# Another order for the end of the kernel stage: the last direct term on GpSimd, weight columns split ahead of the norm and behind it

## The chip, the cores and the metric

One Trainium2 chip, one of its cores. The metric is the device time of one run in microseconds (us); lower is better. The kernel before takes 1165.28 us, the median of three runs (1164.83 to 1167.33).

Engines go by the names of the profile: PE is TensorE (matmul), PEld its weight loads, DVE is VectorE, ACT is ScalarE, POOL is GpSimd, SP is SyncE, which here issues nearly all transfers (DMAs). Each engine works through a queue of its own in order: an instruction that waits holds up all that stand behind it on its engine.

## The reference

Two layers, each of a state-space convolution and a gated feed-forward part, over 2048 positions of 512 channels, with a residual around each part:

```python
def _A_ref(u, A_re, A_im, B_re, B_im, C_re, C_im, log_dt, Dskip):
    dt = jnp.exp(log_dt)[:, None]
    A = A_re + 1j * A_im
    ...
    P = jnp.exp(logdA[:, :, None] * l[None, None, :])
    K = jnp.einsum("dn,dnl,dn->dl", Cc, P, dB).real
    ...
    Yf = Uf * Kf[None, :, :, :]
    ...
    y = (lambda x, *d: x.transpose(*d))(y, 0, 2, 1) + u * Dskip[None, None, :]
    return y
def _B_ref(x, w_gate, w_up, w_down):
    g = _silu(x @ w_gate)
    u = x @ w_up
    return (g * u) @ w_down
x = A_u
x = x + _A_ref(_layernorm(x, axis=-1), ...)
x = x + _B_ref(_layernorm(x, axis=-1), ...)
```

The last two lines stand there twice, for the two layers, with the same parameters. `K` is the convolution's kernel over the 2048 positions, the same for both layers; `u * Dskip` is its direct term.

## The kernel before, in words

The positions are cut into four blocks of 512. The convolution of a block is a product of spectra: a Fourier transform of each block in four groups of frequencies `q` (taken in the order 0, 3, 1, 2) and two halves `h` of the channels, so eight pieces (h, q) per block; block `b` sums the products of its blocks 0 to `b` with the spectra of `K`. The feed-forward part (`ffn`) takes 256 positions at a time, in f16 pairs: every weight is split into a high half and a low half, and each product is three matmuls (lines 909, 910, 912 for gate and up, 924 to 926 for down).

**The kernel stage** comes first (about 0 to 319 us). It makes `K` in eight chunks of 64 channels, and beside it the spectra, the largest column sums of the weights and the first blocks' transforms. Its end, behind the last chunk's matmuls, is written out by hand: inside a `manual_schedule` block the program order is the queue order on ACT, DVE, PE and POOL. The change is in this part. What it consists of:

- `lags` (L491 to L498): the last chunk's matmuls into `pk`. ACT copies them out as `ks` (`spread_in`, L507), PE spreads them into `kp` (`spread_pe`, L523), ACT copies that to the table `kt` (L525), and `skip` (L503) adds the direct term, 64 numbers on one partition, to `kt`. `first_parts` (L580) and `later_parts` (L531, ACT L598/L599, DVE L600, store L538) turn `kt` into spectra.
- `conv[0]`, `conv[1]`: the first block's convolution, one generator per half, five steps and a sixth. Each of the first four steps is one piece q: DVE multiplies (`yk`, L776) and combines (`yf`, L781, L782), PE transforms back (`pi`, L796, eight records of matmuls), and ACT (L748) or DVE (L756, L757) adds pieces up in `bb`. The fifth step makes rows 0 and 1 of the block (L811 to L816), the sixth rows 2 and 3 (L820 to L827). The spectra of half 1 are loaded into `u4` piece by piece (L713), each as soon as `yk` has read the piece of half 0 that lay there.
- `scales()` (L344 to L356, eleven small DVE instructions): from the weights' column sums the powers of two, `sc6`, by which they are split.
- `split(hi, lo, load)`: the split of the weights. `load` issues the next load (L660 for a quarter of the columns of gate or up, 688 KB; L683 and L685 for rows of down), `hi` makes the next high half on ACT (L664; L689 for down), `lo` the next low half on DVE (L669; L692 for down). The quarters come as gate 0, up 0, gate 1, up 1, and so on. A loaded quarter lies in a borrowed buffer until both halves are made; the list `tags` in `split_weights` says in which: `"bt"`, `"n"` or `"xf"`, or a slot 0 to 2 in `wsl[3]`, whose memory the last chunk's matmuls read until they end.
- `norm`: the first feed-forward norm (`first_norm`): statistics on DVE (L203 to L205), a power on POOL (L206), the scaling (L841) on ACT, eight transposes on PE (L843), and the copies L846 (ACT) and L848 (DVE).
- `second(...)`, `direct`: the transform of one piece of the second block for later (16 matmul records at L296, ACT L299, store L300).

Behind the block the order of every engine is set by a scheduler that works from priorities. There the rest of the split stands (`while los`), then for each of the eight (layer, block) pairs the next block's convolution and this one's `ffn`. The first `ffn` multiplies with columns 0 to 255 (f0=0), 256 to 511 (f0=2), and so on; each group's result `pgu` lies in one of two banks of accumulators until ACT (L915, `silu`) and DVE (L916) have read it.

## Time and profile before

| | us |
|---|---|
| median of three runs | 1165.28 |
| the profiled execution | 1163.68 |
| its span in the trace | 1161.5 |
| PE busy in the span | 1099.4 |
| DVE busy | 1000.5 |
| ACT busy | 594.4 |
| POOL busy | 109.1 |
| first matmul of the feed-forward part (L909) | at 318.98 |

A line of the trace's timeline reads: start in us, length in us, engine, line, operation, output and inputs by the program's names, the shapes, the count; in brackets the idle time of the engine just before and what ended it. Instructions of one engine overlap a little, so a line's length is somewhat more than the distance to the next. An f32 matmul stands in the records twice. In a table by stretches each engine's busy time is given with the number of its records, then the granted TensorE clock (1.00 is full), the share of the transfer engines and their GB/s.

### The profile page before, as it was taken

To read this page: it belongs to the slowest core of one execution; us is meant where nothing else is said; L and a number is where in the kernel's file an instruction comes from. 1 tells how busy PE (TensorE), PEld (TensorE's weight loads), DVE (VectorE), ACT (ScalarE), POOL (GpSimd) and SP (SyncE) were. 2 spreads that over 40 slices of the span, in tenths; PEclk is the share of its full clock that TensorE was granted. 3 is DMA by queue.
4 is the path that set the end of the run, shared out by engine and by line. 5 is a ranking of instruction groups with operands and counts; after the bars stand their busy time and mean duration, and the time that the engine had idled before them with its cause. 6 is when DMAs were issued, how large, how long until landed. Compare 5 with 4: busy or idle time off the path is not lost.

```text
span 1161.5 us, 24413 instructions
## 1 busy us (share of the span) xinstructions
PE 1099.4 (95%) x9948; PEld 875.2 (75%) x9948; DVE 1000.5 (86%) x1593; ACT 594.4 (51%) x1194; POOL 109.1 (9%) x162
## 2 busy tenths in 40 slices
PE   1979999998889999999999999999999999999998
PEld 1868888886777868687868687868777686876875
DVE  7999999978889999999899999989994999983212
ACT  6689888833553463557453533655433452334211
POOL 0112222210000010010010000210000010000000
PEclk9989999999989999999999999999999999999999
DMA  5356777766493437332254454342534145312000
GB/s 208 118 148 171 171 176 163 187 184 221 124 290 120 144 119 223 104 111 74 79 154 135 126 162 143 103 131 89 164 110 150 49 121 153 107 42 46 15 24 19
DMA packets 127314, 150.38 MB, mean 129 GB/s; under 512 B 50897, under 2 KB 75985, under 8 KB 127202
## 3 DMA queue, kind: packets, MB, share of 16 engines
q1 hardware_dynamic: 115298, 123.32, 35.0%
q0 software_dynamic: 11904, 25.50, 9.5%
q8 instruction: 78, 1.28, 0.5%
q14 instruction: 34, 0.28, 0.1%
HBM read 98.70 MB, written 33.82 MB: 114 GB/s over the span
## 4 chain that ended last, share of the span: by engine, by line
PE 33%; DVE 26%; issue 8%; DMA 4%; ACT 3%; SPq 1%; POOL 1%; DVEq 0%; ACTq 0%; POOLq 0%
PE pgu L909 6%; PE pgu L910 5%; PE pgu L912 5%; DVE t L776 4%; DVE yk L779 4%; PE py L924 3%; PE py L925 3%; PE py L926 3%; DVE yk L776 3%; DVE z L228 2%; PE pi L796 2%; PE pf L280 2%; DVE sg L916 2%; DVE hl L918 1%; DMA mix<-nn 1%
## 5 line engine op out<-in xcount | busy, mean ns | idle before, releaser
L909 PE MATMUL pgu<-mix,wsl 128*128 128x256 f16 x1280 | 300.1, 274 | 5.5 <-DVE sg L916 4.6
L910 PE MATMUL pgu<-mix,wsl 128*128 128x256 f16 x1280 | 299.7, 274 | 0.0
L912 PE MATMUL pgu<-mix,wsl 128*128 128x256 f16 x1280 | 195.6, 274 | 0.0
L910 PEld LDWEIGHTS <-wsl 128*128 128x128 f16 x1280 | 125.7, 98 | 22.7 <-issue 6.3
L924 PE MATMUL py<-wsl,hh 128*128 128x512 f16 (+1 forms) x352 | 133.4, 379 | 4.7 <-DVE xg L929 3.0
L909 PEld LDWEIGHTS <-wsl 128*128 128x128 f16 x1280 | 125.7, 98 | 16.2
L912 PEld LDWEIGHTS <-wsl 128*128 128x128 f16 x1280 | 125.7, 98 | 15.3
L926 PE MATMUL py<-wsl,hl 128*128 128x512 f16 (+1 forms) x352 | 133.4, 379 | 0.5 <-DVE hl L918 0.5
L925 PE MATMUL py<-wsl,hh 128*128 128x512 f16 x320 | 121.3, 379 | 0.0
L776 DVE TENSOR_TENSOR t<-uu,w 128x1024 f32<-128x1024 f32 x96 | 116.9, 1217 | 3.5 <-DMA w<-wdr 3.3
L915 ACT ACTIVATE sg<-pgu,sc 128x512 f32<-128x512 f32 x80 | 54.6, 683 | 126.5 <-PE pgu L912 123.3
L779 DVE TENSOR_TENSOR yk<-yk,t 128x1024 f32<-128x1024 f32 x96 | 116.8, 1217 | 0.2
L916 DVE SCALAR_TENSOR_TENSOR sg<-pgu,sc,sg 128x512 f32<-128x512 f32 x80 | 59.7, 746 | 52.2 <-ACT sg L915 52.0
L531 PE MATMUL pw<-kt,ek 128*128 128x256 f32 (+1 forms) x384 | 91.0, 374 | 0.0
L917 ACT ACTIVATE hh<-sg 128x512 f16<-128x512 f32 x80 | 50.1, 627 | 77.8 <-DVE sg L916 77.8
L796 PE MATMUL pi<-yl,mix 128*128 128x256 f16 x576 | 78.9, 272 | 0.6 <-DVE yl L228 0.3
L531 PEld LDWEIGHTS pw<-kt,ek 128*128 128x128 f32 x384 | 72.5, 193 | 8.6
L280 PE MATMUL pf<-z,eh 128*128 128x256 f16 x576 | 74.9, 273 | 0.6 <-DVE z L228 0.6
L776 DVE TENSOR_TENSOR yk<-u,w0r 128x1024 f32<-128x1024 f32 x56 | 68.2, 1217 | 0.8 <-ACT u L282 0.8
L918 DVE TENSOR_TENSOR hl<-sg,hh 128x512 f16<-128x512 f32 x80 | 54.9, 686 | 15.5 <-ACT hh L917 15.4
L496 PE MATMUL pk<-re,g 128*32 128x64 f32 x1024 | 61.4, 300 | 6.7 <-DMA g<-g 3.3
L925 PEld LDWEIGHTS <-hh 128*128 128x128 f16 (+1 forms) x352 | 34.4, 98 | 41.5 <-issue 6.0
(237 smaller groups left out, 2162.3 us busy)
## 6 DMA issues: line engine op xcount, KB each, us to landing
w<-wdr SPq DMA_DIRECT2D x96, 256.0 KB, 2.8
uu<-udr SPq DMA_DIRECT2D x96, 256.0 KB, 3.0
udr<-u POOLq DMA_DIRECT2D x32, 256.0 KB, 2.6
g<-g POOLq DMA_DIRECT2D x6, 1024.0 KB, 9.1
udr<-u SPq DMA_DIRECT2D x16, 256.0 KB, 2.9
n<-xdr SPq DMA_DIRECT2D x4, 1024.0 KB, 5.7
kdr<-ks SPq DMA_DIRECT2D x6, 512.0 KB, 2.6
kt<-kdr SPq DMA_DIRECT2D x24, 128.0 KB, 2.9
```

Of the source, the lines that this page charges most:

```text
L280: PE.matmul(pf[:, o], lhsT=e, rhs=m, start=k == 0, stop=k == len(terms) - 1)
L531: PE.matmul(pw[:, i], lhsT=e, rhs=kt[:, :, c + 4 * k0:4 * k1:4, :].rearrange("p g k d -> p k g d"), start=c == 0, stop=c == 3)
L776: V.tensor_tensor(t, uu.unsqueeze(2).to_broadcast([P, NQ, 2, 2, DC]), w.unsqueeze(3).to_broadcast([P, NQ, 2, 2, DC]), OP.mult)
L779: V.tensor_tensor(yk, yk, t, OP.add)
L796: PE.matmul(pi[:, o], lhsT=e, rhs=m, start=k == 0, stop=k == len(terms) - 1)
L909: PE.matmul(o, lhsT=wgu(wi, k, 0)[:, fs], rhs=nh[:, k], start=k == 0, stop=False)
L910: PE.matmul(o, lhsT=wgu(wi, k, 1)[:, fs], rhs=nh[:, k], start=False, stop=False)
L912: PE.matmul(o, lhsT=wgu(wi, k, 0)[:, fs], rhs=nlo[:, k], start=False, stop=k == 3)
L916: V.scalar_tensor_tensor(sg, pgu[:, 1], sc6[:, 4:5], sg, OP.mult, OP.mult)
L924: PE.matmul(py[:, r], lhsT=hh[:n, f, rc], rhs=wd(f, 0)[:n], start=f == 0, stop=False)
L925: PE.matmul(py[:, r], lhsT=hh[:n, f, rc], rhs=wd(f, 1)[:n], start=False, stop=False)
L926: PE.matmul(py[:, r], lhsT=hl[:n, f, rc], rhs=wd(f, 0)[:n], start=False, stop=f == FT - 1)
```

## The change

The calls inside the hand-written part stand in another order. The additions are the same, apart from three things: `skip` of the last chunk goes to POOL (`G`) where it was on DVE (`V`); the second load (up 0) goes to the buffer `"n"`, so that only two loads need the memory of the last chunk's matmuls at first, and `bb1`, which takes the same buffer, is made later; and the eighth piece of `second` is taken inside `conv[1]` where it stood at the end. `scales()` and the first `hi` stand ahead of everything, gate 0 and up 0 are finished before the third step of `conv[0]`, and the low halves of gate 1 to up 3 stand behind the norm's statistics.

```diff
-        tags = iter(("bt", 0, 1, 2, "bt", 0, 1, 2, "n", "xf", "bt"))
+        tags = iter(("bt", "n", 0, 1, "bt", 2, 0, 1, "n", "xf", "bt"))
...
+        split(0, 0, 1)
         load_x(xs[0], 0, 0)
-        split(0, 0, 3)
+        split(0, 0, 2)
...
+        scales()
+        split(1, 0)
         ks = spread_in(pk)
...
-        bb1 = tl([P, 2, 2, 2, HD], "bb1", "n")
         norm = first_norm(tl([P, 2, D], "nn1", "hf"))
-        take(conv[0], 1)
-        spread_pe(ks, kts[1])
-        skip(c, kts[1], V)
-        take(conv[0], 1)
-        scales()
-        split(1, 0)
-        first_parts(c, 0)
-        take(conv[0], 1)
-        split(1, 1)
-        split(0, 0, 1)
-        first_parts(c - 1, 3)
+        last = second(*sec[-1])
         split(1, 0)
         take(conv[0], 1)
-        first_parts(c - 1, 1)
-        split(1, 0)
-        take(conv[1], 1)
-        first_parts(c, 2)
-        take(conv[1], 1)
+        split(0, 1)
+        split(0, 0, 1)
+        spread_pe(ks, kts[1])
+        skip(c, kts[1], G)
+        take(conv[0], 1)
         split(0, 1)
         split(0, 0, 1)
         take(conv[0], 1)
+        first_parts(c, 0)
+        split(1, 0)
+        bb1 = tl([P, 2, 2, 2, HD], "bb1", "n")
+        first_parts(c - 1, 3)
+        take(conv[0], 1)
+        first_parts(c - 1, 1)
         take(conv[1], 1)
-        split(1, 1)
-        split(0, 0, 1)
+        first_parts(c, 2)
+        split(1, 0)
         take(conv[1], 1)
-        split(0, 1)
-        split(0, 0, 1)
+        take(conv[0], 1)
+        take(conv[1], 1)
+        split(1, 0)
+        take(last, 2)
+        take(conv[1], 1)
         take(odd, 2)
         take(conv[1], 1)
         take(norm, 1)
+        split(0, 0, 1)
+        split(0, 1)
+        split(0, 0, 1)
         take(rest, 2)
...
         take(rest, 4)
+        split(0, 1)
         split(0, 0, 3)
         sizes(c, kts[1], ks)
         direct_size()
         nn2 = tl([P, 2, D], "nn2", "nn")
-        take(second(*sec[-1]), 2)
```

How this moves instructions is seen at three places. The first is DVE's queue from the last store of spectra (`wo`, L563) on, before:

```order
L563 TENSOR_TENSOR wo<-pw,wo 128x2x6x64
L776 TENSOR_TENSOR yk<-mix,w0r 128x1024
L781 TENSOR_TENSOR yf<-yk 128x256
L782 TENSOR_TENSOR yf<-yk 128x256
L503 TENSOR_TENSOR kt_438<-kt_438,tdk 1x4x16
L776 TENSOR_TENSOR yk<-mix,w0r 128x1024
L781 TENSOR_TENSOR yf<-yk 128x256
L782 TENSOR_TENSOR yf<-yk 128x256
L344 TENSOR_REDUCE c_2727<-cmx 128x3
```

and in the change, from the last instruction of `scales()` on, which now follow L563 at once:

```order
L356 TENSOR_SCALAR sc_92<-bits 128x6
L776 TENSOR_TENSOR yk<-mix,w0r 128x1024
L781 TENSOR_TENSOR yf<-yk 128x256
L782 TENSOR_TENSOR yf<-yk 128x256
L669 SCALAR_TENSOR_TENSOR wsl_2674<-st_2542,sc_92,wsl_2674 128x2x344
L669 SCALAR_TENSOR_TENSOR wsl_2675<-st_2542,sc_92,wsl_2674 128x2x344
L776 TENSOR_TENSOR yk<-mix,w0r 128x1024
L781 TENSOR_TENSOR yf<-yk 128x256
L782 TENSOR_TENSOR yf<-yk 128x256
L669 SCALAR_TENSOR_TENSOR wsl_2676<-st_2678,sc_92,wsl_2675 128x4x344
L776 TENSOR_TENSOR yk<-mix,w0r 128x1024
```

L503 is gone from DVE, and between the first, second and third piece of the convolution the low halves of gate 0 and up 0 are made.

The second place is PE's queue at the end of `conv[1]`; `pi` are its transforms, `pf` the sixteen matmuls of the eighth piece of `second`. The difference (a count of 4 is one piece):

```order
 L580 MATMUL pw<-kt_438,ef 128x64 x2
 L580 MATMUL pw<-kt_438,ek_84 128x64 x6
-L796 MATMUL pi<-yf,mix 128x256 x12
+L796 MATMUL pi<-yf,mix 128x256 x8
+L296 MATMUL pf<-n_1635,ef 128x256
+L296 MATMUL pf<-n_1635,ek_84 128x256
+L296 MATMUL pf<-n_1637,ek_84 128x256 x2
+L296 MATMUL pf<-n_1635,ef 128x256
+L296 MATMUL pf<-n_1635,ek_84 128x256
+L296 MATMUL pf<-n_1637,ek_84 128x256 x2
+L796 MATMUL pi<-yf,mix 128x256 x4
```

The `pf` matmuls now stand ahead of the convolution's last `pi`; before, they stood just ahead of the first matmul of the feed-forward part.

The third place is ACT's queue where the split of down (L689) meets the first `silu` (L915), set by the scheduler. Before:

```order
L222 ACTIVATE mv<-mv,epst 128x2
L689 ACTIVATE wsl_2677<-st_3036,sc_92 128x512 x4
L689 ACTIVATE wsl_2677<-st_3038,sc_92 128x512 x2
L689 ACTIVATE wsl_2677<-st_3038,sc_92 96x512
L860 ACTIVATE nn_3045<-xg,rs 128x512
L689 ACTIVATE wsl_2676<-st_3034,sc_92 128x512 x3
L689 ACTIVATE wsl_2677<-st_3034,sc_92 128x512
L915 ACT_TABLE_LOAD
L915 ACTIVATE sg_3081<-pgu,sc_92 128x512
```

and in the change:

```order
L689 ACTIVATE wsl_2677<-st_3051,sc_92 128x512 x2
L689 ACTIVATE wsl_2677<-st_3051,sc_92 96x512
L222 ACTIVATE mv<-mv,epst 128x2
L915 ACT_TABLE_LOAD
L915 ACTIVATE sg_3082<-pgu,sc_92 128x512
L689 ACTIVATE wsl_2677<-st_3049,sc_92 128x512 x4
L689 ACTIVATE wsl_2676<-st_3047,sc_92 128x512 x3
L689 ACTIVATE wsl_2677<-st_3047,sc_92 128x512
L915 ACTIVATE sg_3082<-pgu,sc_92 128x512
```

The first `silu` stood behind eleven high halves of down and now stands behind three. DVE's queue follows: ahead of its first L916 stood eleven low halves L692 and both L776 and L779 of the next block's first `k=1` term, and now three L692 and the L776. Further back the scheduler's order of the five engines differs in places up to matmuls that lie at about 598 us in the trace of before; from there to the end the rows of both programs are the same.

## The prediction

> **What bounds the kernel now.** I read the windows first: who is busy where.
>
> ```profile
> 260.00:280.00 20.00, 17.01 (x144) 14.25 (x137) 13.48 (x30) 7.89 (x9) 0.00 (x0) 0.91 0.82 287
> 280.00:300.00 20.00, 16.92 (x80) 14.40 (x79) 19.52 (x32) 5.25 (x10) 0.00 (x0) 0.83 0.45 132
> ...
> 340.00:440.00 100.00, 98.93 (x795) 74.69 (x794) 96.24 (x166) 44.89 (x89) 8.74 (x11) 1.00 0.45 134
> 440.00:545.00 105.00, 103.98 (x897) 83.64 (x895) 102.77 (x188) 55.91 (x109) 10.15 (x16) 1.00 0.40 126
> ```
>
> From 340 to 545 us PE idles 2.1 us (1.07 + 1.02) and DVE 6.0 us (3.76 + 2.23): both are full, and time won ahead of 340 stays won only if both win it. The end of the kernel stage, 260 to 334, is another matter. Next, therefore, PE's rows there; the bracket is its idle time and who ended it.
>
> ```profile
> 262.78 1.93 PE L523 MATMUL kp<-ks,ident 128*32 128x256 f32 x32
> 267.70 3.45 PE L796 MATMUL pi<-yf,mix 128*128 128x256 f32 x8 [2.99 <-DVE yf L781]
> ...
> 272.94 1.95 PE L796 MATMUL pi<-yf,mix 128*128 128x256 f32 x8
> ...
> 283.48 1.95 PE L796 MATMUL pi<-yf,mix 128*128 128x256 f32 x8
> 287.74 3.02 PE L796 MATMUL pi<-yf,mix 128*128 128x256 f32 x8 [2.31 <-DVE yf L781]
> 291.52 3.75 PE L796 MATMUL pi<-yf,mix 128*128 128x256 f32 x8 [0.77 <-ACT bb L748]
> ...
> 303.93 1.36 PE L843 MATMUL pt<-ident,nn 128*128 128x128 f32 x8 [3.33 <-ACT nn L841]
> 305.12 0.49 PE L531 MATMUL pw<-kt,ef 128*128 128x192 f32 x2
> ...
> 315.53 0.59 PE L296 MATMUL pf<-n,ef 128*128 128x256 f32 x2
> ...
> 318.98 0.27 PE L909 MATMUL pgu<-mix,wsl 128*128 128x256 f16 x1
> ...
> 333.97 0.37 PE L909 MATMUL pgu<-mix,wsl 128*128 128x256 f16 x1 [4.34 <-DVE sg L916]
> ```
>
> Five gaps, 13.7 us. Behind some of them matmuls take 1.6 to 1.9 times as long (`pi` 3.45, 3.02, 3.75 against 1.95). DVE's rows say why PE waits.
>
> ```profile
> 255.32 1.22 DVE L776 TENSOR_TENSOR yk<-mix,w0r 128x1024 f32<-128x1024 f32 x1
> ...
> 256.92 0.42 DVE L782 TENSOR_TENSOR yf<-yk 128x256 f32<-128x256 f32 x1
> 265.84 0.21 DVE L503 TENSOR_TENSOR kt<-kt,tdk 1x64 f32<-1x64 f32 x1 [8.51 <-ACT kt L525]
> ...
> 267.90 0.15 DVE L344 TENSOR_REDUCE c<-cmx 128x3 f32<-128x6 f32 x1
> ...
> 269.56 1.22 DVE L776 TENSOR_TENSOR yk<-mix,w0r 128x1024 f32<-128x1024 f32 x1
> ...
> 280.62 1.65 DVE L669 SCALAR_TENSOR_TENSOR wsl<-wsl,sc,wsl 128x1376 f16<-128x1376 f32 x1
> ...
> 301.08 0.17 DVE L205 TENSOR_SCALAR rs<-mv 128x2 f32<-128x2 f32 x1
> 301.17 1.78 DVE L669 SCALAR_TENSOR_TENSOR wsl<-st,sc,wsl 128x688 f16<-128x688 f32 x2
> ...
> 307.00 0.56 DVE L600 TENSOR_TENSOR wos<-pw,wos 128x384 f32<-128x384 f32 x1 [3.51 <-ACT wos L599]
> 308.96 0.56 DVE L600 TENSOR_TENSOR mix<-pw,mix 128x384 f32<-128x384 f32 x1 [1.40 <-ACT mix L599]
> ...
> 312.59 0.41 DVE L820 TENSOR_TENSOR bb<-bb 128x256 f32<-128x256 f32 x1
> ...
> 325.37 2.06 DVE L692 SCALAR_TENSOR_TENSOR wsl<-st,sc,wsl 128x512 f16<-128x512 f32 x3
> ...
> 333.17 0.75 DVE L916 SCALAR_TENSOR_TENSOR sg<-pgu,sc,sg 128x512 f32<-128x512 f32 x1
> ...
> 340.73 1.23 DVE L776 TENSOR_TENSOR t<-uu,w 128x1024 f32<-128x1024 f32 x1 [2.55 <-DMA w<-wdr]
> ```
>
> L503, 0.21 us of work, waits for ACT's `kt` and shuts DVE for 8.51 us while work that needs no `kt` stands behind it. From 312.59 DVE is full to its L916 at 333.17, for which PE waits 4.34 us.
>
> **The change part by part**, against the profiled execution (1163.68 us; the median of the runs shown is 1.6 us above it). ACT's rows:
>
> ```profile
> 261.02 1.02 ACT L507 ACTIVATE ks<-pk 128x1024 f32<-128x1024 f32 x1 [6.61 <-PE pk L497]
> ...
> 264.78 1.02 ACT L525 ACTIVATE kt<-kp 128x1024 f32<-128x1024 f32 x1 [1.30 <-PE kp L523]
> ...
> 269.73 1.44 ACT L664 ACTIVATE wsl<-st,sc 128x1376 f16<-128x1376 f32 x1 [3.93 <-DVE sc L356]
> ```
>
> *DVE's 8.51 us are filled.* From 255.4 on: `scales` 1.7 us (267.90 to 269.56), first piece 2.0 (255.32 to 257.34), gate 0's low half 1.7, second piece 2.0: `yf` at 262.8. PE then goes from `kp`, which ends at 264.71, straight into `pi` two. DVE waits 0.7 us for up 0's high half (ACT: L507 ends 262.04, plus 1.44), makes its low half (1.6), and the third piece is there at 267.1. On PE seven pieces, `pi` and L580 in turn, take 272.94 to 285.43, 1.78 us each. So: `pi` two to 266.5, nine pieces from 267.1 to 283.1, the moved `pf` 3.45 us (315.53 to 318.98), the last `pi` 1.95: end at 288.5, where it was 295.27. **The shift is 6.8 us**, with the 3.45 us of `pf` already done. DVE has 27.5 us of work to do meanwhile, is done at 285, and waits 3.5 us for that `pi`.
>
> *POOL's skip and the loads* hide behind this. No trace shows such an addition on POOL; the nearest rows:
>
> ```profile
> L223 POOL TENSOR_TENSOR rs<-mv,mhalf 128x2 f32<-128x2 f32 x15 | 24.6, 1637 | 176.1 <-ACT mv L222 176.1
> ...
> L206 POOL TENSOR_TENSOR rs<-rs,mhalf 128x4 f32<-128x4 f32 x2 | 2.0, 1020 | 33.0 <-DVE rs L205 33.0
> ```
>
> Bounds 0.2 us (DVE's price) and 1.64; I take 1.02, since it is as small an operation. `kt` is then there at 266.0 to 267.5; L580 wants it at 268.9, after `pi` three. Either end costs nothing; above 3 us PE waits. Behind it in POOL's queue stands only the norm's L206, wanted some 27 us later. The Trainium skill speaks against the move: "SBUF — State Buffer", Terms, says that VectorE and GpSimd share a port pair which one holds for its full instruction while the other is blocked. By that rule the addition could start up to one L776 (1.22 us) late, at worst to 268.7, still in time.
>
> Loads: four quarters and two blocks of x are now asked for within about 3 us of 261.
>
> ```profile
> L660 SPq DMA_DIRECT2D wsl<-in_B_w_up_dram x4: 383/460/1420, 261.4 to 295.7; - x4
> ...
> DMA to landing us min/median/max: 4.1/7.2/9.9
> ```
>
> At the longest, 9.9, gate 1 lands at 271.3; ACT takes it about 271.4. Up 0, asked for at 251.5, must be there at 262.0: 10.5 us. The same 9.9 for `u4`'s second piece, asked for at 263.1, gives 273.0, when DVE wants it at 272.7: I count 0.3. Later the loads of gate 3 and up 3 wait in SP's queue for the low halves of gate 1 and up 1 (about 296 and 298); behind them stand the stores of the L600, none of which is ready before 298, so nobody loses by it.
>
> *The norm.* L205, L669, L841 and L843 follow each other as before, so the transposes move by 6.9 us to 297.0 (L843 was 303.93), the eight L531 groups behind them still take 10.4 (305.12 to 315.53), and with `pf` gone the first L909 starts at **308.6 instead of 318.98**.
>
> *The first silu.* DVE reaches L600 at 302.0 (308.96 less 6.9) and, past L848, gate 2's low half and one L600, the block's second rows at 305.7 (as long as before, 3.6, since gate 2 replaces up 2). From there to L916 it took 20.6 (312.59 to 333.17); now up 2 is added (1.6), and eight L692 (0.67 each, 5.4), L779 (1.1) and 0.7 of small rows and waits fall away: 15.0. L916 runs at 320.7 to 321.4. PE, with two groups of 5.24 us done by 319.1, waits 2.3 us and starts f0=4 at **321.4 instead of 333.97, 12.5 us earlier**. ACT is in time: its three L689 and the table load fit ahead of 320.
>
> What such a gap does to the clock differs from case to case; the figure behind the counts of records is the granted clock:
>
> ```profile
> 304.00:306.00 2.00, 1.95 (x14) 1.72 (x15) 0.00 (x0) 1.25 (x2) 0.00 (x0) 1.00 0.82 199
> ...
> 334.00:336.00 2.00, 2.00 (x10) 1.44 (x10) 2.00 (x5) 1.88 (x3) 0.00 (x0) 0.50 1.64 170
> ```
>
> After the 4.34 us it was 0.50, after the 3.33 us ahead of the transposes 1.00. A cold start of f0=4 would cost up to about 2.6 us (half of 5.24). The Trainium skill's "TensorE: Matmul & The Clock Gate", Part 1, says that the clock halves after an idle window of about 3.4 us, so that by it a gap of 2.3 us stays warm; the trace doesn't bear it out, since 2.31 us of idle were followed by a `pi` of 3.02. The sum below holds with either, since PE isn't what sets it.
>
> *DVE sets it.* DVE idled 8.51 + 3.51 + 1.40 + 0.30 + 2.55 = 16.3 us from 257.3 to 340.7 (the 0.30 ahead of the first L692). Now: 0.7 + 0.3 + 3.5 (the last `pi`) + 3.5 (the two L600 at 300 and 302) + 1 (the load of `w`; 0 to 2.55, nearer the low end because it stands ahead of two 1 MB loads in SP's new order) = 9.0. With 0.2 of L503 gone, **DVE is 7.5 us ahead at 341**, PE 12.5. Both then have a fixed amount of work up to where the orders meet again (598 us), and PE can't pass DVE, whose `yf` it needs. One debt: ahead of the norm row L862 at 524 DVE's new queue holds one L916, one `yl`, two `z` and one `yf` pair more, 0.7 each, less L503:
>
> ```profile
> 524.02 0.68 DVE L862 TENSOR_TENSOR nn<-nn 128x512 f16<-128x512 f32 x1
> ```
>
> If PE waits for that row, 2.5 us go back: 5.0 to 7.5 won. I take the middle, 6.3: 1157.4 for the profiled execution, and 1165.28 − 6.3 = **1159.0** for the median.
>
> **The rivals.**
> - *PE sets it* (DVE makes good its lag, because its 6.0 us of idle up to 545 vanish): the whole 12.5 us, 1152.8. For it: PE's rows from 437 to 500 carry the chain of waits. Against: DVE's 96% and 98%.
> - *The gain is handed back in the middle*: PE, 5 us ahead of DVE, waits for several `yf` and each wait slows the matmuls behind it. One gap like that at 267.70 costs 2.99 + 1.5 = 4.5 us; two of them, less the 5 us of lead, leave 2.3 of the 6.3 won, and a w load as late as before (1.5 more) leaves under 1: 1163 to 1165.
> - *Slower*: PE runs cold again and again between 341 and 545. Each such wait costs 4.5 us as at 267.70; PE's lead over DVE covers 5 us of them in all. It decides from the third: 3 × 4.5 − 5 − 6.3 = +2.2, 1167.5; four make it 1172. For it: PE comes further ahead of DVE than it was, so it meets each `yf` sooner. Against: only 2.1 us of PE idle in that stretch before, so the new order would have to be much worse.
>
> **How the numbers follow.** Forecast (5 to 9 won) 0.55, PE sets it 0.15, handed back 0.15, slower 0.15. The first two and a small part of the third are faster by over 0.2% (2.3 us, about what a measurement can tell): 0.72; within it 0.13; slower 0.15. The range reaches from PE's 1152.5 to the handed-back end, 1165.5, and leaves out the slower case.
>
> **What would show it.** Right: no L503 on DVE, no gap ahead of `pi` two, first L909 near 308.6, f0=4 near 321.4 after 2 to 3 us, DVE's first `t` L776 near 332, the same distance to the end from 598 on. Wrong: a gap ahead of L580 (POOL over 3 us), ACT or DVE waiting for a load at 271 to 283, or PE idle over 7 us between 341 and 545.

## The result and the profile after

The change makes the kernel slower by a little: 1169.49 us, the median of eleven runs (1166.80 to 1173.23), against 1164.83 us for the kernel before in eleven runs beside it (1163.96 to 1167.61). The ratio is 1.0035 with a 95% interval of 1.0022 to 1.0048. The profiled execution of the change took 1166.85 us (span 1164.9), at the low end of its runs; it stands 3.2 us above the profiled execution of before.

At its own place the change does what it says. These are DVE's rows from the end of the kernel stage on, where before stood the 8.51 us wait of L503; the bracket is the wait and what ended it.

```profile
263.26 1.65 DVE L669 SCALAR_TENSOR_TENSOR wsl<-st,sc,wsl 128x1376 f16<-128x1376 f32 x1 [0.80 <-ACT wsl L664]
264.83 1.22 DVE L776 TENSOR_TENSOR yk<-mix,w0r 128x1024 f32<-128x1024 f32 x1
...
270.64 1.22 DVE L776 TENSOR_TENSOR yk<-mix,w0r 128x1024 f32<-128x1024 f32 x1 [0.35 <-ACT w0r L581]
...
274.49 1.23 DVE L776 TENSOR_TENSOR yk<-mix,w0r 128x1024 f32<-128x1024 f32 x1 [1.83 <-DMA mix<-udr]
...
289.34 0.69 DVE L756 TENSOR_TENSOR bb<-bb,pi 128x512 f32<-128x512 f32 x1 [2.49 <-PE pi L796]
...
300.80 0.56 DVE L600 TENSOR_TENSOR wos<-pw,wos 128x384 f32<-128x384 f32 x1 [1.95 <-ACT wos L599]
304.03 0.56 DVE L600 TENSOR_TENSOR mix<-pw,mix 128x384 f32<-128x384 f32 x1 [2.67 <-ACT mix L599]
...
333.00 1.23 DVE L776 TENSOR_TENSOR t<-uu,w 128x1024 f32<-128x1024 f32 x1 [0.42 <-DMA w<-wdr]
339.64 0.69 DVE L862 TENSOR_TENSOR nn<-nn 128x512 f16<-128x512 f32 x1 [3.03 <-DMA mix<-nn]
```

The long wait is gone, but the brackets still add up to 13.5 us, against 16.3 before. PE now goes from `kp` straight into two `pi`, and comes to the feed-forward part (L909) 8.0 us and to its second pair of groups (the L909 behind the wait for `sg`) 10.5 us earlier:

```profile
262.57 1.94 PE L523 MATMUL kp<-ks,ident 128*32 128x256 f32 x32
264.44 4.12 PE L796 MATMUL pi<-yf,mix 128*128 128x256 f32 x16
...
287.35 1.89 PE L796 MATMUL pi<-yf,mix 128*128 128x256 f32 x8
...
297.72 1.36 PE L843 MATMUL pt<-ident,nn 128*128 128x128 f32 x8 [3.29 <-ACT nn L841]
...
299.48 2.13 PE L531 MATMUL pw<-kt,ek 128*128 128x192 f32 x6
...
303.53 1.14 PE L531 MATMUL pw<-kt,ek 128*128 128x192 f32 x6
...
311.01 0.27 PE L909 MATMUL pgu<-mix,wsl 128*128 128x256 f16 x1
...
323.47 0.27 PE L909 MATMUL pgu<-mix,wsl 128*128 128x256 f16 x1 [1.81 <-DVE sg L916]
```

The windows show where it is lost again. Three stretches of the kernel stage, then the two that were quoted of before:

```profile
260.00:280.00 20.00, 19.87 (x168) 16.99 (x159) 16.47 (x27) 8.29 (x12) 0.53 (x1) 1.00 0.84 288
280.00:300.00 20.00, 15.49 (x81) 13.68 (x80) 15.86 (x28) 6.39 (x11) 1.34 (x1) 0.98 0.22 68
300.00:304.00 4.00, 4.00 (x19) 4.00 (x18) 0.56 (x1) 2.83 (x11) 0.00 (x0) 0.70 0.97 273
340.00:440.00 100.00, 91.80 (x667) 66.10 (x668) 92.45 (x160) 39.82 (x82) 6.90 (x11) 0.95 0.43 128
440.00:545.00 105.00, 102.54 (x871) 81.90 (x869) 100.35 (x179) 53.42 (x104) 9.51 (x14) 0.98 0.43 125
```

From 340 to 545 us PE is busy 194.3 us where it was 202.9, and DVE 192.8 where it was 199.0. Two full engines have become two that wait: DVE idles 12.2 us where it idled 6.0, for ACT (6.0 us), loads and transposing transfers (3.7) and POOL (1.7), and only 0.5 for PE. PE's gaps there end mostly with DVE (L781, L228, L929):

```profile
342.59 0.70 PE L796 MATMUL pi<-yf,mix 128*128 128x256 f32 x2 [2.71 <-DVE yf L781]
...
422.68 0.58 PE L924 MATMUL py<-wsl,hh 128*128 128x512 f16 x1 [1.31 <-DVE xg L929]
...
485.94 0.38 PE L924 MATMUL py<-wsl,hh 128*128 128x512 f16 x1 [2.25 <-DVE xg L929]
...
486.85 0.63 PE L925 MATMUL py<-wsl,hh 128*128 128x512 f16 x1
```

To compare kernels whose orders differ I measure, in the profiled executions, from ACT's L507 (the copy `ks`, at 261 us) to three DVE rows: the second L862 (a norm row), the fifteenth L779 behind the block, and the ninth L929 (a block's end, where the orders have met).

| us behind L507 | second L862 | fifteenth L779 | from one to the other | ninth L929 |
|---|---|---|---|---|
| before | 80.86 | 178.07 | 97.21 | 338.75 |
| the change | 78.76 | 180.68 | 101.92 | 342.72 |

The change is 2.1 us ahead at the first marker, 2.6 behind at the second, 4.0 behind at the third. From there to the end of the span both take the same, 561.7 and 561.3 us. So the hand-written block is worth about 2 us at the first marker, and behind it the change loses about 6, nearly as much as DVE's extra 6.2 us of idle time. That it is the scheduler's new order that loses them is a guess here; e1 and e2 below show it.

### The profile page after: what moved, and what is told of

It reads as the page before. It is cut to its first block, busy times and chain, and to the rows that moved or that the text cites. A ratio compares the mean times of both kernels' runs of the same rounds, so it can differ in the third digit from the quotient of the medians.

```text
span 1164.9 us, 24407 instructions
## 1 busy us (share of the span) xinstructions
PE 1100.4 (94%) x9948; PEld 873.8 (75%) x9948; DVE 1001.2 (86%) x1592; ACT 594.4 (51%) x1194; POOL 108.2 (9%) x163
## 4 chain that ended last, share of the span: by engine, by line
DVE 39%; PE 38%; issue 13%; DMA 7%; ACT 1%; POOL 1%; SPq 1%; DVEq 0%; POOLq 0%; ACTq 0%
DVE t L776 5%; PE pgu L909 5%; PE pgu L910 5%; PE pw L531 5%; PE pgu L912 5%; DVE yk L779 4%; DVE z L228 3%; DVE yk L776 3%; PE py L924 3%; PE py L925 3%; PE py L926 3%; PE pk L496 2%; DMA g<-g 2%; PE pk L497 2%; PE pi L796 2%
## 5 line engine op out<-in xcount | busy, mean ns | idle before, releaser
L909 PE MATMUL pgu<-mix,wsl 128*128 128x256 f16 x1280 | 299.5, 273 | 5.2 <-DVE wmax L615 1.8
L910 PE MATMUL pgu<-mix,wsl 128*128 128x256 f16 x1280 | 299.3, 273 | 0.0
L912 PE MATMUL pgu<-mix,wsl 128*128 128x256 f16 x1280 | 196.1, 273 | 0.0
L910 PEld LDWEIGHTS <-wsl 128*128 128x128 f16 x1280 | 125.2, 98 | 22.5 <-issue 6.4
L909 PEld LDWEIGHTS <-wsl 128*128 128x128 f16 x1280 | 125.1, 98 | 16.5
L912 PEld LDWEIGHTS <-wsl 128*128 128x128 f16 x1280 | 125.1, 98 | 15.1
L776 DVE TENSOR_TENSOR t<-uu,w 128x1024 f32<-128x1024 f32 x96 | 117.0, 1219 | 3.5 <-DMA w<-wdr 3.3
L915 ACT ACTIVATE sg<-pgu,sc 128x512 f32<-128x512 f32 x80 | 54.6, 683 | 124.4 <-PE pgu L912 119.8
L779 DVE TENSOR_TENSOR yk<-yk,t 128x1024 f32<-128x1024 f32 x96 | 117.0, 1218 | 0.2
L916 DVE SCALAR_TENSOR_TENSOR sg<-pgu,sc,sg 128x512 f32<-128x512 f32 x80 | 59.7, 746 | 54.3 <-ACT sg L915 54.1
L531 PE MATMUL pw<-kt,ek 128*128 128x256 f32 (+1 forms) x384 | 92.2, 378 | 0.0
L531 PEld LDWEIGHTS pw<-kt,ek 128*128 128x128 f32 x384 | 73.8, 196 | 8.6
L280 PE MATMUL pf<-z,eh 128*128 128x256 f16 x576 | 74.9, 273 | 0.9 <-DVE z L228 0.9
L776 DVE TENSOR_TENSOR yk<-u,w0r 128x1024 f32<-128x1024 f32 x56 | 68.2, 1218 | 2.8 <-ACT u L282 2.7
L918 DVE TENSOR_TENSOR hl<-sg,hh 128x512 f16<-128x512 f32 x80 | 54.9, 687 | 16.3 <-ACT hh L917 16.1
```

The lines of the kernel that those rows point to most:

```text
L280: PE.matmul(pf[:, o], lhsT=e, rhs=m, start=k == 0, stop=k == len(terms) - 1)
L531: PE.matmul(pw[:, i], lhsT=e, rhs=kt[:, :, c + 4 * k0:4 * k1:4, :].rearrange("p g k d -> p k g d"), start=c == 0, stop=c == 3)
L776: V.tensor_tensor(t, uu.unsqueeze(2).to_broadcast([P, NQ, 2, 2, DC]), w.unsqueeze(3).to_broadcast([P, NQ, 2, 2, DC]), OP.mult)
L779: V.tensor_tensor(yk, yk, t, OP.add)
L909: PE.matmul(o, lhsT=wgu(wi, k, 0)[:, fs], rhs=nh[:, k], start=k == 0, stop=False)
L910: PE.matmul(o, lhsT=wgu(wi, k, 1)[:, fs], rhs=nh[:, k], start=False, stop=False)
```

## The experiments

To part the block from the order, most kernels fix the order behind the block by a table: per engine, edges without a semaphore link the instructions in the wanted queue order, so that the scheduler has no choice and no instruction waits for anything new.

```diff
+    mark = len(nc.cur_bb.bb.instructions)
     pscale = product_scale()
...
+    put_in_order(tc, nc.cur_bb.bb.instructions[mark:])
+def put_in_order(tc, insts):
...
+                tc.add_manual_dep(insts[at], prev, mybir.DependencyInfo(
+                    mybir.DependencyClass.NoSync, mybir.DependencyReason.DATA), reason="order")
```

"Old order" is that of the kernel before behind the block, "new order" that of the change. The theories go by letters in the expectations: **A**, the block's lead is real and the new order behind it loses it; **B**, PE's lead over DVE turns into waits and slow matmuls in any order; **C**, 1 MB loads of x, which the new order puts ahead of awaited transfers, hold these up; **D**, DVE sets the end, and a lead of PE is worth nothing; **E**, PE's gaps and the slow clock behind them are the cost; **F**, the cost lies in the rows of PE, DVE, ACT and POOL between about 337 and 440 us. Ratios are to the kernel before on the same chip (medians of 1166.12 to 1166.65 us), with 95% intervals.

### The block and the order apart

**e1: the change's block, old order behind it.**

```diff
 block: as in the change
-order behind: new
+order behind: old
```

> The hand-written block of the change, and behind it the order of every engine exactly as in the kernel before. Theory A (the lead is real, the scheduler's new order behind the block loses it): the first f0=4 matmul at about 323.5 us as in the change, PE idle at most 3 us between 341 and 600, 1158 to 1161 us. Theory B (PE and DVE are both full there, so that PE's lead over DVE turns into cold waits in whatever order): PE idle over 7 us between 341 and 600, 1165 to 1170 us, as the change has.

1162.49 us, 0.9966 (0.9950 to 0.9982): faster, by 4 us. The block is good; the order behind it is what costs. The time lies 1.5 us above the range that I had given theory A, and f0=4 comes at 333.83, not at 323.5: PE's whole lead runs into one wait, since the old order has DVE's first `sg` late:

```profile
333.83 0.37 PE L909 MATMUL pgu<-mix,wsl 128*128 128x256 f16 x1 [9.82 <-DVE sg L916]
```

A 10 us lead of PE, lost in one gap, in a kernel that is faster than before: this is for D.

**e2: the block of before, new order behind it.**

```diff
 block: as before
-order behind: old
+order behind: new
```

> The hand-written block of the kernel before, and behind it the order of every engine exactly as in the change. Theory A: the start as before (f0=4 at about 334 us), then PE idle 6 us or more between 341 and 600, against 2.5 before, and 1168 to 1174 us. Theory B: there is no lead to turn into waits, PE idle at most 4 us, 1163 to 1166 us.

1179.60 us, 1.0107 (1.0090 to 1.0124), more than theory A's 1168 to 1174. With e1 and the result this makes a square:

| ratio | old order behind | new order behind |
|---|---|---|
| block of before | 1 | 1.0107 |
| block of the change | 0.9966 | 1.0035 |

The new order costs 8 us (0.69%) behind the change's block and 12 behind that of before, where a wait of DVE for `uu`, 6.2 us at 331, is part of it. A holds.

**e3: only `skip` on GpSimd.** Nothing else is moved by hand.

```diff
-        skip(c, kts[1], V)
+        skip(c, kts[1], G)
```

> The kernel before with the last direct term on GpSimd and nothing else; the order behind the block stays that of before. DVE's 8.51 us stall at 257.3 goes, PE's 2.99 us gap at 267.70 and the slow transforms behind it (1.5 us) with it, so the first L909 comes about 4.5 us earlier, at 314.5 us. Theory A: with the old order behind it the gain is kept, 1160 to 1162 us. Theory B: it is handed back in the middle, 1163 to 1166 us.

1161.68 us, 0.9963 (0.9950 to 0.9976), as fast as e1. One word does what the whole block does: L503 leaves DVE's queue, the scheduler keeps its order behind the block (DVE and ACT row for row, PE but for four `pi` matmuls), and L909 starts 3.0 us earlier behind L507. It doesn't win the 8.51 us either, for the next wait takes over:

```profile
266.84 0.94 DVE L669 SCALAR_TENSOR_TENSOR wsl<-st,sc,wsl 128x688 f16<-128x688 f32 x1 [4.14 <-ACT wsl L664]
```

**e12: the change's block with `skip` left on DVE, old order behind it.**

```diff
-        skip(c, kts[1], G)
+        skip(c, kts[1], V)
```

> The change with the last direct term back on DVE (behind the low half of gate 0, where the change has it on GpSimd) and the old order behind the block. DVE comes there about 264.5 us, ACT's kt is ready at 265.8, so it waits 1 to 2 us where before it waited 8.51. If the filling of the stall is what counts, and not the engine: within 1.5 us of the run with the change's block and the old order, 1161.5 to 1164 us. If GpSimd's part counts by itself: 1165 us or more.

1166.15 us, 0.9999 (0.9987 to 1.0010). Without GpSimd the rearranged block is worth nothing. I had expected L503 to wait 1 to 2 us; it waits 5.12:

```profile
265.32 0.21 DVE L503 TENSOR_TENSOR kt<-kt,tdk 1x64 f32<-1x64 f32 x1 [5.12 <-ACT kt L525]
```

### Which part of the order

**e5 and e6: the order cut at 440 us.** On the change's block: e5 has the new order up to about 440 us and the old one behind, e6 the reverse.

```diff
-order behind: new
+order behind (e5): new for 909 PE, 191 DVE, 92 ACT, 82 SP, 11 POOL rows, then old
+order behind (e6): old up to there, then new
```

> The block of the change, behind it the order of the change up to about 440 us (past the fourth L929) and the order of before from there. In the traces the stretch from the fourth to the ninth L929 took 161.3 us with the old order in three kernels and 163.6 to 166.1 us with the new one in three. If each stretch costs what its order costs, whatever comes ahead of it (theory A), the second stretch goes back to 161 to 162 us and the kernel stands at 1164 to 1167 us, 3 to 5 us below the change. If the second loss was the late effect of the first stretch, it stays at 164 to 166 us and the time at 1168 to 1170 us.

> The block of the change, behind it the order of before up to about 440 us and the order of the change from there. Theory A: the first stretch as in the old-order run (the fourth L929 about 176.3 us behind the ACT copy L507 of the last chunk), the second 164 to 166 us, 1165 to 1168 us, some 4 us above the run with the old order throughout. If the second loss was the late effect of the first stretch: 161 to 162 us there, and 1161 to 1163 us.

e5: 1173.50 us, 1.0064 (1.0039 to 1.0089), above both ranges expected. e6: 1164.24 us, 0.9978 (0.9965 to 0.9991). The cost comes from the rows ahead of 440. What is lost behind 440 is a late effect of them: from the fourth to the ninth L929 e5 takes 165.3 us with the old rows, as long as the change (165.3), and e6 with the new ones takes 162.4 (before: 161.3).

**e17 and e18: cut at 337 us too.** On the change's block: e17 has the new order to 337 us and the old one behind; e18 the old one to 337, the new one to 440, the old one behind.

```diff
-order behind: new
+order behind (e17): new for 128 PE, 24 DVE, 21 ACT, 13 SP, 2 POOL rows, then old
+order behind (e18): old up to there, new to the cut of e5, then old
```

> The change's block and the change's order up to about 337 us (24 rows of DVE, two silu done), the old order from there. Theory F with the loss behind 337 us: like the run with the first silu early, f0=4 at about 323.5 us, the stretch to the fifteenth L779 at 97 us, 1160 to 1163 us. If the early silu themselves cost the time (the half-empty banks come too early for what follows): 1167 us or more.

> The change's block, the old order up to about 337 us, the change's order from there to about 440, the old order behind it. Theory F: the first silu are late as in the run with the old order (PE waits 9 to 10 us for f0=4, so that PE has no lead over DVE), and the stretch to the fifteenth L779 still takes 101 us or more: 1168 to 1175 us. If PE's lead from the early silu is what makes the waits (theory B): the stretch at 97 to 98 us, 1161 to 1164 us.

e17: 1164.68 us, 0.9983 (0.9971 to 0.9994). e18: 1177.79 us, 1.0104 (1.0086 to 1.0122). The new order's rows between 337 and 440 us carry the cost: F as to the place. The size is off: both times lie above the ranges given (1160 to 1163, 1168 to 1175), and e18 is 16 us (1.38%) behind e1, twice what the whole new order costs behind this block. A seam between two orders may cost something too, so the cuts show where the cost lies better than how large it is. e18 also settles B. There PE has no lead, for it loses it ahead of 337 as in e1, and the gaps behind come all the same:

```profile
333.90 0.37 PE L909 MATMUL pgu<-mix,wsl 128*128 128x256 f16 x1 [9.53 <-DVE sg L916]
...
424.73 0.81 PE L796 MATMUL pi<-yl,mix 128*128 128x256 f16 x6 [2.33 <-DVE yl L228]
430.27 0.58 PE L924 MATMUL py<-wsl,hh 128*128 128x512 f16 x1 [2.67 <-DVE xg L929]
```

e17 has the early f0=4 of the change, behind the same 1.8 us gap, and then waits 5.18 us for `yf` at 332.79: what PE wins at the first silu it gives back within ten us.

**e16: SP's queue alone as before.** The change's block and order on the other four engines; SP in the old order.

```diff
-order behind on SP: new
+order behind on SP: old
```

> The change with the order of SP's transfers behind the block as in the kernel before; PE, DVE, ACT and POOL in the change's order. If the place of the transfers is what the new order loses by (theory C): DVE's waits for w and for the transposing transfers fall under 1 us each, 1161 to 1165 us. If it is the rows of the engines themselves (theory F: loops through PE, ACT, POOL and DVE with too little work between their links): the stretch from the second L862 to the fifteenth L779 stays at 101 us or more, 1168 to 1173 us.

1173.81 us, 1.0063 (1.0048 to 1.0078). Not better: the transfers then come in an order that the engines' new rows don't want, and `w` is waited for 5.85 us at 342.5. The gap of 2.33 us ahead of the eleven `pi` stays, at 2.32. So the order of the transfers isn't shown to be the cause by itself; but with a new wait of 5.85 us the run doesn't part SP's queue cleanly from the other four, and the reverse, SP new and the others old, wasn't run.

The stretch between the first two markers sorts the kernels the same way: 96.9 to 97.7 us with the old rows there (before, e1, e3, e6, e7, e12, e17; 98.5 and 99.4 in e9 and e8 below, whose first marker is early), 101.9 to 105.2 with the new ones (the change, e2, e5, e16, e18). The variants of the new order in the next section take 100.8 (e11) to 110.7 (e4).

### The waits, one by one

**e4: the loads of x later.** The change, with `n` (L232) behind the fourth L864 of SP's queue and `xf` (L232) behind its first L933. Of the rows:

```diff
-L232 DMA xf<-in_A_u_dram 128x4x512
-L232 DMA n<-in_A_u_dram 128x4x512
 L864 DMA_TRANSPOSE mix<-nn_3058 128x4x128 x2
 L774 DMA uu<-udr_114 128x512
 L716 DMA u<-udr_114 128x512
 L864 DMA_TRANSPOSE mix<-nn_3058 128x4x128
+L232 DMA n<-in_A_u_dram 128x4x512
 L772 DMA w<-wdr 128x512
...
 L933 DMA xdr<-xg 128x512
+L232 DMA xf<-in_A_u_dram 128x4x512
```

> The change, every queue in its order, but two 1 MB loads of x moved back in SP's queue: that into n behind the fourth transposing transfer L864, that into xf behind the first store L933; neither is read before 375 us. Theory C (these loads hold up the transposing transfers for which DVE's second L862 waits 3.03 us, and PE behind it 2.71 us and cold): the wait at 339.64 falls under 0.7 us, PE's gap at 342.6 under 0.7 us, and 3 to 5 us are won there. If that is what cost the lead, 1164 to 1166 us; if the order loses it again later (theory A), 1167 to 1169 us. If the loads don't matter, the wait stays at 3 us and the time at 1169 to 1170 us.

1174.75 us, 1.0072 (1.0051 to 1.0093): worse than the change. The 3.03 us of L862 go, and DVE waits for `w` three times. The first of these loads stands behind `n` now and the third behind `xf`; the second is asked for late, behind four L890, and lands as fast as usual:

```profile
346.49 1.23 DVE L776 TENSOR_TENSOR t<-uu,w 128x1024 f32<-128x1024 f32 x1 [3.47 <-DMA w<-wdr]
...
357.39 1.23 DVE L776 TENSOR_TENSOR t<-uu,w 128x1024 f32<-128x1024 f32 x1 [2.90 <-DMA w<-wdr]
...
372.74 1.23 DVE L776 TENSOR_TENSOR t<-uu,w 128x1024 f32<-128x1024 f32 x1 [4.32 <-DMA w<-wdr]
```

`w` (256 KB) lands up to 7.8 us after it is asked for, where 2.8 is usual. C is right that a load of x holds up what stands behind it, and wrong that moving it wins time.

**e8: the load in four pieces, in before.** `skip` on GpSimd, old order; `n` of block (0, 2) as four loads behind awaited ones.

```diff
-            load_x(n, layer, b)
+            load_x(n, layer, b) if (layer, b) != (0, 2) else [nc.sync.dma_start(n[:, c], x[0, b * T + c * P:b * T + (c + 1) * P, :]) for c in range(4)]
```

> The kernel before with the last direct term on GpSimd and the old order, and the 1 MB load of x into n, which stood just ahead of the 256 KB load of w that DVE awaits for 2.77 us at 338, cut in four loads of 256 KB that stand later in SP's queue, each behind a transfer that is awaited. Theory C (a 1 MB load delays the awaited transfer behind it): the wait for w falls under 0.8 us, DVE's later waits for w stay under 1 us, and 1.5 to 2.5 us are won against the skip alone: 1159 to 1160.5 us. If the transfer engines were not what w waited for: a wait of over 2 us, and 1161 to 1163 us.

1161.20 us, 0.9953 (0.9941 to 0.9965). The wait for `w` (2.77 us in e3) is gone, but little comes of it, where I had expected 1.5 to 2.5 us: the ratio is 0.10% (1.2 us) below e3's 0.9963, which lies inside the interval.

**e10 and e11: the same in the new order.** e10 has the change's block and order with `n` and `xf` in four pieces, each behind awaited transfers; in e11, besides, two loads of `w` stand ahead of four L890, and L224 five rows later on DVE.

```diff
-            nc.sync.dma_start(xt, x[0, b * T:(b + 1) * T, :].rearrange("(c p) d -> p c d", p=P))
+            [nc.sync.dma_start(xt[:, c:c + k], x[0, b * T + c * P:b * T + (c + k) * P, :].rearrange("(c p) d -> p c d", p=P)) for k in ((1,) if b == 2 else (4,)) for c in range(0, 4, k)]
```
```diff
 L779 TENSOR_TENSOR yk<-yk,t 128x1024
-L224 SCALAR_TENSOR_TENSOR rs<-mv,rs 128x2
 L781 TENSOR_TENSOR mix<-yk 128x256
 L782 TENSOR_TENSOR mix<-yk 128x256
 L776 TENSOR_TENSOR t<-uu,w 128x1024
 L228 SCALAR_TENSOR_TENSOR z_3083<-z_3083 128x2x256
 L228 SCALAR_TENSOR_TENSOR bb<-pi,sy,bb 128x512
+L224 SCALAR_TENSOR_TENSOR rs<-mv,rs 128x2
```

> The change with its own order, and the two 1 MB loads of x (into n and xf) cut in four of 256 KB each that stand one by one behind awaited transfers in SP's queue. Theory C: DVE's second L862 no longer waits (3.03 us), and no wait for w is over 1.2 us up to 400 us, unlike the run with the loads moved whole (3.47, 2.90, 4.32); the second L862 at 75.5 to 76.5 us behind L507, 2 to 3 us won against the change, 1165.5 to 1168 us. If every such transfer only moves the wait: 1169 us or more.

> The run before with two more waits taken out of the change's order: two loads of w (L772) go ahead of the four transposing transfers L890 that they stood behind, and the small DVE row L224, which waits 1.68 us for POOL's L223 at 434 us, goes five rows back. Theory D/A (what the new order costs between 340 and 441 us are DVE's own waits): the stretch from the second L862 to the fifteenth L779, 101.9 us in the change and 97.2 before, comes down to 98 to 99.5 us and the time to 1162 to 1165 us. If PE's cold gaps set it instead, the stretch stays at 101 us or more and the time where the run with the loads in four stands.

e10: 1170.75 us, 1.0043 (1.0029 to 1.0058). e11: 1171.12 us, 1.0042 (1.0023 to 1.0060). Both as the change: e10 trades the wait of L862 for one of 3.01 us on `w` at 353.98, and e11 the wait of L224 for a gap of PE. Its stretch between the first two markers, expected at 98 to 99.5 us, is 100.8:

```profile
436.75 0.27 PE L796 MATMUL pi<-yl,mix 128*128 128x256 f16 x1 [3.83 <-ACT yl L785]
```

**e13, e14, e15: PE's gaps.** This is the loop in which PE's first large gap behind 350 us arises in the change, all engines:

```profile
412.89 1.47 PE L280 MATMUL pf<-z,eh 128*128 128x256 f16 x12
...
413.19 2.09 DVE L228 SCALAR_TENSOR_TENSOR bt<-n 128x256 f32<-128x256 f32 x6
...
414.42 0.38 PE L925 MATMUL py<-wsl,hh 128*128 128x512 f16 x1
...
414.56 0.58 ACT L282 ACTIVATE u<-pf 128x512 f32<-128x512 f32 x1
...
415.19 1.22 DVE L776 TENSOR_TENSOR yk<-u,w0r 128x1024 f32<-128x1024 f32 x1
...
416.33 0.74 DVE L228 SCALAR_TENSOR_TENSOR yl<-mix,sy,yl 128x512 f16<-128x512 f32 x1
...
417.13 1.36 PE L796 MATMUL pi<-yl,mix 128*128 128x256 f16 x11 [2.33 <-DVE yl L228]
```

PE waits for `yl`, which on DVE stands behind six `bt` and a `yk`, which waits for ACT's `u`, which PE itself made with L280. In before about 2.9 us of gate and up matmuls (L909, L910, L912) stand between that L280 and this `pi`; in the new order two `py` do. e13 puts `yl` ahead on DVE, and two L929 that PE waits for later; e14 puts the next seven `py` ahead of the `pi` on PE; e15 is e10, e13 and e14 together.

```diff
 L627 TENSOR_SCALAR sy<-sy 128x1
+L228 SCALAR_TENSOR_TENSOR yl_3084<-mix,sy,yl_3084 128x512
 L228 SCALAR_TENSOR_TENSOR bt<-n 128x256 x6
 L776 TENSOR_TENSOR yk<-u,w0r 128x1024
-L228 SCALAR_TENSOR_TENSOR yl_3084<-mix,sy,yl_3084 128x512
...
-L776 TENSOR_TENSOR t<-uu,w 128x1024
 L929 SCALAR_TENSOR_TENSOR xg<-py,sc_92,xg 128x512
+L776 TENSOR_TENSOR t<-uu,w 128x1024
```

> The change with three rows of DVE's queue moved a few places ahead, all else in its order: the row yl (L228) for which PE waits 2.33 us at 417 goes ahead of the six bt rows and of yk, one L929 (422) ahead of a t L776, one L929 (485) ahead of an L779 and a bb row. DVE has the same work. Theory E (PE's fixed gaps and the slow clock behind them are the cost of the new order): the gaps of 2.33, 1.31 and 2.25 us fall under 0.3, 1.0 and 0.8, with them some 4 us of half-speed matmuls behind the first and third, and 4 to 7 us are won against the change: 1163 to 1166 us. Theory D (DVE sets the end): PE's gaps go, but DVE's fifteenth L779 and later L929 stay within 1 us, and the time at 1168 to 1171 us.

> The change with one move in PE's queue, all else in its order: the eleven pi matmuls (L796) that wait 2.33 us at 417 go behind the next seven py matmuls, to the end of that row of py. PE then has work while DVE makes yl, and the pi lie where PE waited 1.31 us for L929. Theory E: both gaps come to under 1 us each and the slow clock from 418 to 425 goes, 3 to 5 us are won: 1165 to 1167 us. Theory D: 1168 to 1171 us.

> The moves of the last two runs together, and the two 1 MB loads of x in four each, which takes out DVE's wait for the transposing transfers at 339.6 and PE's 2.71 us at 342.6 behind it. Theory E: PE's idle time from its first L909 to the ninth L929, 15.5 us in the change, comes under 9 us, and the time to 1161 to 1164 us, near the run with the old order. Theory D: not under 1167 us.

e13: 1169.96 us, 1.0035 (1.0022 to 1.0047). e14: 1174.06 us, 1.0071 (1.0049 to 1.0093). e15: 1171.58 us, 1.0049 (1.0033 to 1.0065). None better than the change. e13 and e14 take the gap ahead of that `pi` out, and the next link has one; here e14, PE:

```profile
421.07 0.61 PE L926 MATMUL py<-wsl,hl 128*128 128x512 f16 x1 [3.27 <-DVE hl L918]
...
444.99 0.37 PE L796 MATMUL pi<-yl,mix 128*128 128x256 f16 x1 [5.34 <-ACT yl L785]
```

Six kernels (e4, e10, e11, e13, e14, e15) took waits of the new order out, and in each another came up. PE's idle time from its first L909 to the ninth L929 didn't fall in e13, e14 and e15: 15.8 us in the change, 16.9, 21.3 and 19.4 in them. So what falls is that single gaps can be taken out for a gain, as E had it; that PE's idle time as a whole is the cost isn't refuted by these runs, since none lowered it.

### A better version

**e7: the change's block, old order, the first silu early.** The first two L915 (ACT) and L916 (DVE) stand ahead of most L692. DVE:

```diff
 L614 TENSOR_TENSOR sy<-sy,dmax 1x1
+L916 SCALAR_TENSOR_TENSOR sg_3082<-pgu,sc_92,sg_3082 128x512
 L692 SCALAR_TENSOR_TENSOR wsl_2677<-st_3049,sc_92,wsl_2677 128x512 x2
...
 L779 TENSOR_TENSOR yk<-yk,t 128x1024
-L916 SCALAR_TENSOR_TENSOR sg_3082<-pgu,sc_92,sg_3082 128x512
```

> The block of the change with the old order behind it, and there only the first two silu (ACT L915) and their L916 on DVE moved ahead of most low halves L692, so that PE need not wait 9.82 us for f0=4. Theory D (DVE sets the end, PE's lead is worth nothing): PE's gap ahead of f0=4 falls under 4 us and f0=4 starts 6 to 9 us earlier, but DVE's second L862 and every L929 from the second on stay within 0.7 us, and the time is that of the old-order run, 1161 to 1163.5 us. If PE sets it: 1154 to 1158 us.

1161.39 us, 0.9952 (0.9938 to 0.9965). f0=4 starts at 322.64, 11.2 us earlier than in e1, behind a gap of 0.37, and PE loses what it won at the next thing that it needs from DVE:

```profile
322.64 0.28 PE L909 MATMUL pgu<-mix,wsl 128*128 128x256 f16 x1 [0.37 <-DVE sg L916]
...
333.34 1.22 PE L796 MATMUL pi<-yf,mix 128*128 128x256 f32 x2 [7.03 <-DVE yf L781]
```

Between e1 and e7 the ratios differ by 0.14%, 1.6 us, and the intervals overlap: little or nothing is left of the 11. D is not quite borne out: in the profiled executions DVE is 1.2 us earlier at its second L862 and 1.9 at the ninth L929, where D allowed 0.7.

**e9: e7 with the four loads of e8.**

```diff
-            load_x(n, layer, b)
+            load_x(n, layer, b) if (layer, b) != (0, 2) else [nc.sync.dma_start(n[:, c], x[0, b * T + c * P:b * T + (c + 1) * P, :]) for c in range(4)]
```

> Both of the last cures at once: the block of the change, the old order behind it with the first two silu and L916 early, and the load of x into n in four. Theory D (PE and DVE are both full behind 340 us, the later of the two sets the end): with the skip alone DVE was 2.6 us earlier at its second L862 once the wait for w was gone, but PE, which idled 0.8 us in that stretch, then held it back; here PE is 4 to 5 us earlier too, so that both leads count: the second L862 at 75.5 to 76.5 us behind L507, the fifteenth L779 at 172 to 173.5, and 1158 to 1160 us. If DVE alone set it already, or the wait for w only moves: L779 at 174 to 175 us, and 1160.5 to 1162 us.

1160.51 us, 0.9959 (0.9943 to 0.9975), not the 1158 to 1160 expected if both leads counted. e3, e7, e8 and e9 can't be told apart; all four beat the kernel before by 0.4 to 0.5%, and with it the change. The cheapest is e3, one word.

## Why the prediction was wrong, step by step

- *DVE's stall filled, the `pi` moved up*: right. Two `pi` stand behind `kp` without a gap, and the last `pi` ends at 289.2 (predicted 288.5).
- *POOL's skip*: right, and smaller than the value taken: 0.53 us (1.02 taken, bounds 0.2 and 1.64), with nobody waiting for it. `kt` was ready at 265.60; the addition starts at 265.69, in the middle of a DVE L776, and ends 0.17 us behind the end of that L776 (266.05). So it is in all fifteen traces in which it starts under an L776: the end is 0.17 us behind the L776's each time, and the addition takes 0.48 to 0.61 us, the longer the more of the L776 is left. In e3 and e8, where no DVE instruction runs beside it, it takes 0.31. The L776 keeps its 1.22 us. By the Trainium skill ("SBUF — State Buffer", Terms) VectorE and GpSimd share a port pair, and one is blocked while the other holds it. The traces agree: the addition is held up by some 0.2 us, which lie inside its own length and cost nothing. The change and e3:

```profile
265.69 0.53 POOL L503 TENSOR_TENSOR kt<-kt,tdk 1x64 f32<-1x64 f32 x1 [16.17 <-ACT kt L525]
...
265.56 0.31 POOL L503 TENSOR_TENSOR kt<-kt,tdk 1x64 f32<-1x64 f32 x1 [16.16 <-ACT kt L525]
```

- *The loads*: too small. I counted 0.3 us for `u4`'s second piece; DVE waited 1.83, at 274.49, which was one of the signs of being wrong. It was asked for at 265.10, not at 263.1, because SP took 0.5 to 1.5 us for each of the four quarters ahead of it, and landed 9.3 us later. In the other profiled executions with this block the same wait is 1.8 to 4.0 us; with the block of before there is none.
- *The norm and the transposes*: right, 297.72 (297.0). First L909 at 311.01 (308.6), 1.7 us of it because the eight L531 behind the gap ran slowly at first: 2.13 us for six matmul records at 299.48, 1.14 at 303.53, granted clock 0.70 from 300 to 304. Before, nearly the same gap (3.33) was followed by full clock; the last section shows why.
- *The first silu*: right, and 2.1 us late. DVE's L916 at 322.68 (320.7 to 321.4), f0=4 at 323.47 (321.4), gap 1.81 (2.3).
- *"DVE is 7.5 us ahead at 341"*: mis-sized. The waits came to 13.5 us where I summed 9.0: `u4` 1.8 for 0.3, the two L600 4.6 for 3.5, L862 3.03 for nothing, the last `pi` 2.5 for 3.5, the load of `w` 0.4 for 1. DVE is 2.1 us ahead at L862.
- *The step that failed*: "Both then have a fixed amount of work up to where the orders meet again", with a debt of at most 2.5 us. The amount of work is the same; the idle time in it isn't. The new order costs 4.7 us from the second L862 to the fifteenth L779 (101.92 less 97.21) and 1.4 more to the ninth L929: 2.1 − 4.7 − 1.4 = −4.0. I had read the order at the places where rows move and taken the 205 us behind them for full because they were full before. e1 and e2 show that the order costs this, and e5, e6, e17 and e18 that its rows from 337 to 440 do.
- *DVE sets the end, PE's 12.5 us are worth nothing by themselves*: right, or nearly (e7 left at most 2 us of 11). PE's rows show it with gaps of 9.82, 7.03 and 5.18 us that give a lead back.
- *The rivals*: the sign and the symptom (PE idle over 7 us between 341 and 545: 9.7) were those of the rival "slower", its mechanism not. It came from PE's lead over DVE; e18 has the cost without the lead, e1 the lead without the cost.

**What stays open.** Shown is that the new order behind the block costs 8 us behind the change's block and 12 behind that of before, and that its rows between about 337 and 440 us, on all five queues together, carry the cost. Which link of it is the root isn't: in six kernels the wait only moved, and no run gave one of the engines alone the new order. That loops such as the one at 412 to 417 hold too little work between their links is read from the trace and not shown by a run, since the runs that eased single links won nothing. Why the scheduler chose this order wasn't tried.

## What to carry to other kernels

Where a hand-written part feeds a scheduler, an edit to it redraws the order of everything behind, and the redraw can cost more than the edit wins; fix the old order behind the edit and time the two apart before you judge either. A stall that is filled is worth what the next waits leave of it (4 of 8.5 us here by e1 and e3, since the loads, the next `pi` and ACT came due), and a lead of an engine that needs the bounding engine's result within ten us was worth at most 2 of 11 us (e7). Try the smallest part of a rearrangement alone: one word had the whole gain, and left the order behind nearly as it was.

## What the runs showed of the hardware

- After nearly the same gap ahead of the transposes the clock differed: full after 3.33 us in before, 0.70 over 300 to 304 after 3.29 us in the change, and in e1, after 3.30 us, 0.50 there. What decides is how the gap lies in a grid. In all twenty traces the granted clock is either full or half and changes only at steps of 3.41 us. From 90 us on, a step at full clock in which PE was idle for more than about 2 us was followed by one at half clock, and one with less than 1.7 us of idle time never was. In the change (first two lines) 2.2 us of the gap lie in one step, and the next is at half; in before (last two) the gap is cut into 1.6 and 1.8 us, and the clock stays full. The first figure behind a step's length is PE's busy time, the clock is the third from the end:

```profile
295.60:299.01 3.41, 1.24 (x9) 1.00 (x10) 3.25 (x5) 1.52 (x2) 0.89 (x1) 1.00 0.23 54
299.01:302.42 3.41, 3.41 (x13) 3.41 (x12) 0.56 (x1) 3.12 (x7) 0.00 (x0) 0.50 0.96 276
...
298.79:302.21 3.42, 1.80 (x12) 1.50 (x10) 3.28 (x9) 0.00 (x0) 0.87 (x1) 1.00 0.14 51
302.21:305.62 3.41, 1.64 (x12) 1.41 (x13) 1.28 (x3) 1.81 (x3) 0.48 (x1) 1.00 0.39 91
```

- Shorter gaps are enough if they lie in one step: the 2.25 us at 485.94 do, the step ends at 486.74, and the `py` matmuls take 0.38 us at first and 0.63 from 486.85 on, nearly a microsecond after work had begun again. The Trainium skill ("TensorE: Matmul & The Clock Gate", Part 1) has the clock halve after an idle window of about 3.4 us that runs freely. The traces agree with the length and with the free run, and show that the window need not be idle throughout.
- A transfer of 1 MB ahead of one of 256 KB in the same queue delayed the small one to 7.8 us from issue to landing, from a usual 2.8 (e4); in four pieces put behind awaited loads it no longer delayed the one at 338 (e8).
